# Sliding-window attention and a multiplicative FFN: Q and K cast by DMA, transposed in 32x32 blocks by VectorE, scores as 32-row matmuls

## The chip, the core and the metric

One Trainium2 chip, one core of it. The metric is the device time of one launch in microseconds: 290.55 us before the change, the median of three runs (290.41 to 290.74). Lower is better.

## What is computed

The reference takes q, k and v of shape (8, 8, 576, 64), that is 8 batches, 8 heads, 576 positions and 64 columns a head, and four weights, all in float32:

```
scores = (q @ k^T) / 8, kept where 0 <= i - j < 64, else -1e9   # causal, window of 64
attn   = softmax(scores)
x      = (attn @ v), heads side by side: 4608 tokens x 512
a, b   = x @ w1, x @ w2                                          # 512 -> 1024 each
out    = ((a * b) @ w3) @ w_out                                  # 1024 -> 1024 -> 512
```

## The kernel before, in words

**Fold.** `w3 @ w_out` is one 1024x512 matrix, `wc_sb`, made once on the chip: `fold_t(fc)` transposes 128 rows of w3 on TensorE (L470), VectorE copies them out (L472), `fold_mm(fc)` multiplies (L478). There are eight such steps.

**FFN.** The 4608 tokens are cut into nine groups g of 512. A group has twelve *slots*: `ffn_ab(g, fc)` for fc 0 to 7, which makes a 128-row piece of a and of b with 8 matmuls of 512 columns (L414), has ScalarE copy a out of PSUM (L419) and VectorE multiply b by it (L420); and `ffn_o(g, t)` for t 0 to 3, 8 matmuls (L432), a VectorE copy (L434) and a store.

**Attention.** Heads go in pairs j (0 to 3); the two heads of a pair are called a or hh (0, 1). The 576 queries of a batch are cut into three segments si of 192. A *unit* d is a batch, a segment and two of the four pairs: 48 units. `scores(d)` makes key-by-query scores with 8 matmuls (L279), each with 64 rows: the 64 columns of head a lie in one half of the 128 partitions. ScalarE's exp (L283) follows, and two masks on GpSimd (POOL, L291 and L293), which zero what lies outside the window; in segment 0 there are four smaller ones. `values(d)` multiplies by V with a block of ones beside it, which gives the softmax denominators (L336; L320 for the first two batches), takes the reciprocal by Ln and Exp on ScalarE (L342 to L344, or L326 and L327) and multiplies on VectorE into `xT` (L345 and L346, or L328), the FFN's input.

**Q and K.** `load_qk` loads both as float32 from SP's queue into `stage`. `cast_qk` makes float16 of them (L215, mostly on POOL; `cast_third`, L222, for the first batch). `transposes` then transposes 128x128 blocks on TensorE, six to a group (L254), and VectorE, or ScalarE for one in six, copies each group out of PSUM (L258). V and the weights are cast on their way by DMAs issued from POOL (L234, L453, L457, L463).

**PSUM.** It has eight banks: one for transposes (`ps_t`), two for scores (`ps_s`), two for `values` (`ps_v`), three for the FFN and the fold (`ps_f`).

**Order.** It is written by hand, and each engine works in that order. The *start* is a straight list: the first batches' loads, dummy matmuls (`keep_busy`, L503), the fold, the attention of batches 0 and 1, the FFN's group 0 and the transposes of batch 2. The *loop* then runs the remaining 96 slots. Between slots it runs *ticks* u, twelve to a batch; a tick comes when the next slot's due time, reckoned from what the group needs, allows it: one tick to a slot for most groups, 1.5 slots to a tick for groups 1, 4 and 7. In a tick, even u runs `scores(u/2)`, odd u runs `values` of the unit before, and the table `late` adds loads, casts, transposes and V copies for the coming batches:

```
    late = {0: [("t", 1, "k", 0), ("cast", 1, "q", 0)], 1: [("cast", 1, "q", 1)],
            2: [("t", 1, "k", 1), ("load", 2, "k")], 4: [("t", 1, "k", 2), ("v", 1, 0, 2, 3)],
            5: [("load", 2, "q")], 6: [("t", 1, "q", 0), ("v", 1, 4, 5)], 7: [("cast", 2, "k", 0)],
            8: [("t", 1, "q", 1), ("copy", 1, 4)], 9: [("copy", 1, 1), ("cast", 2, "k", 1)], 10: [("t", 1, "q", 2)]}
```

Of the kernel before, what the change touches and what calls it, by code (L numbers as in the profile page):

```python
# [15 lines left out]
P = 128  # L16
# [128 lines left out]
def kernel(  # L145
# [18 lines left out]
    TP, TI = 32, 18  # L164
# [4 lines left out]
    ND = 6 * B  # L169
# [29 lines left out]
    raws, k16s, q16s = {}, {}, {}  # L199

    def load_qk(b, which, gate=None):
        src = k if which == "k" else q
        t = sb.tile([P, 2, TI * D], FP32, name="stage", bufs=4)
        if gate is not None:
            gate(t[:, 0, 0:1], 0.0)
        for hh in range(2):
            nc.sync.dma_start(out=t[:, hh], in_=src[b, hh:H:2].rearrange("j (p r) d -> p j (r d)", r=TI))
        raws[which, b] = t

    def cast_qk(b, which, hh, cp):  # L210
        t = raws[which, b]
        if hh == 0:
            (k16s if which == "k" else q16s)[b] = sb.tile([P, TI, P], FP16, name=which + "16", bufs=1)
        t16 = (k16s if which == "k" else q16s)[b]
        cp(t16[:, :, hh * D:hh * D + D], t[:, hh].rearrange("p (i d) -> p i d", d=D))  # L215

    def cast_third(b, which, c, cp):
        t = raws[which, b]
        if c == 0:
            (k16s if which == "k" else q16s)[b] = sb.tile([P, TI, P], FP16, name=which + "16", bufs=1)  # L220
        t16 = (k16s if which == "k" else q16s)[b]
        cp(t16[:, 6 * c:6 * c + 6].rearrange("p i (hh d) -> p hh i d", hh=2),  # L222
           t[:, :, 6 * c * D:6 * c * D + 6 * D].rearrange("p hh (i d) -> p hh i d", d=D))
# [19 lines left out]
    kTs, qTs = {}, {}  # L243

    def transposes(b, which, *cs, into=None, cps=None):

        t16, dst = (k16s, kTs) if which == "k" else (q16s, qTs)
        if cs[0] == 0:
            dst[b] = sb.tile([P, NJ, S], FP16, name=which + "T")
        if into is None:  # L250
            into = [ps_t.tile([P, 6, P], FP16, name="tp")]
        for c, tp in zip(cs, into):
            for i in range(6):
                nc.tensor.transpose(tp[:, i, :], t16[b][:, 6 * c + i, :], ident16)  # L254
        if cps is None:
            cps = [dve_cp if which == "k" or c != 1 else act_cp for c in cs]
        for c, tp, cp in zip(cs, into, cps):
            cp(dst[b].rearrange("q j (p i) -> q j p i", i=TI)[:, :, :, 6 * c:6 * c + 6],  # L258
               tp.rearrange("q i (p j) -> q j p i", p=TP))


# [3 lines left out]
    def scores(d):  # L265

        b, r = divmod(d, 6)
        si, jp = divmod(r, 2)
# [3 lines left out]
        s_ps = ps_s.tile([P, 2, 2, 256], FP32, name="s_ps")  # L272
        for jj in range(2):
            j = 2 * jp + jj
            c0 = 0
            for (k0, q0, n, _) in seg:
                for a in range(2):
                    half = slice(a * D, a * D + D)
                    nc.tensor.matmul(s_ps[:, a, jj, c0:c0 + n], kT[half, j, k0:k0 + P], qT[half, j, q0:q0 + n],  # L279
                                     start=True, stop=True, skip_group_check=True)  # L280
                c0 += n
        pt = sb.tile([P, 2, 2, 256], FP16, name="pt", bufs=3)
        nc.scalar.activation(pt[:, :, :, 0:w], s_ps[:, :, :, 0:w], AF.Exp, bias=-SHIFT, scale=scale)  # L283

        rows = pt.rearrange("k a j n -> k (a j) n")
# [11 lines left out]
    def values(d):  # L297
# [7 lines left out]
        o_ps = ps_v.tile([P, 2, 512], FP32, name="o_ps")  # L305
# [6 lines left out]
        if b < SHORT:  # L312

            for jj in range(2):
                c0 = 0
                for bi, (k0, q0, n, _) in enumerate(seg):
                    o0 = jj * 192 + q0 - q_base
                    for e in range(2):
                        for a in range(2):
                            nc.tensor.matmul(o_ps[a * D:a * D + D, e, o0:o0 + n],  # L320
                                             v16[:, si * 2 + bi, j0 + jj, (2 * a + e) * D:(2 * a + e) * D + D],
                                             pt[:, a, jj, c0:c0 + n],
                                             start=(jj == 0 and bi == 0), stop=(bi == 1), skip_group_check=True)
# [6 lines left out]
        for jj in range(2):  # L330
            first = True
            for a in range(2):
                c0 = 0
                for bi, (k0, q0, n, _) in enumerate(seg):
# [3 lines left out]
                                     pt[:, a, jj, c0:c0 + n],  # L338
# [9 lines left out]
    def keep_sums(n):  # L348
# [5 lines left out]
    late = {0: [("t", 1, "k", 0), ("cast", 1, "q", 0)], 1: [("cast", 1, "q", 1)],  # L354
# [3 lines left out]

    def event(b, kind, ahead, *a):
        if b + ahead >= B:  # L360
            return
        if kind == "load":
            load_qk(b + ahead, *a)
        elif kind == "cast":
            cast_qk(b + ahead, *a, pool_cp)
        elif kind == "t":
            transposes(b + ahead, *a)
        elif kind == "v":
            load_v(b + ahead, *a)
        else:  # L370
            copy_v(b + ahead, *a)

    LAG = 3

    def tick(u):

        b, r = divmod(u, 12)
        d = u // 2
        if u % 2 == 0 and d < ND:
            scores(d)  # L380
        ev = late.get(r, [])
        for e in ev:
            if e[0] == "t":
                event(b, *e)
        if u % 2 == 1 and 12 <= d - 1 < ND:
            values(d - 1)
        for e in ev:
            if e[0] != "t":
                event(b, *e)
        n, m = divmod(u - LAG - 4, 4)  # L390
        if m == 3 and n >= 6:
            keep_sums(n)

# [100 lines left out]
    def count_bad():  # L494
        c_ps = ps_t.tile([1, 1], FP32, name="tp")
# [3 lines left out]
    def keep_busy(n):  # L499

        d = ps_t.tile([P, P], FP32, name="tp")
# [4 lines left out]
    load_qk(0, "k")  # L506
    load_qk(0, "q")
# [6 lines left out]
    ones_of(0)  # L514
    ones_of(1)
    load_wo()
    load_w3(0)
    load_v(0, 0, 2, 3)
    for n in range(1, 4):
        load_w3(n)  # L520
    load_v(0, 4, 5)
# [8 lines left out]
    def spare(pool, name):  # L530

        t = pool.tile([P, 2, 1024], FP16, name=name)
        return [t[:, i, 0:768].rearrange("p (i n) -> p i n", i=6) for i in range(2)]

    keep_busy(75)
    tps = spare(ps_s, "s_ps") + spare(ps_v, "o_ps")
    for c in range(3):
        cast_third(0, "k", c, act_cp if c == 1 else dve_cp)
# [156 lines left out]
```

## Time and profile before

| what | us |
|---|---|
| median of three runs | 290.55 |
| span of the profiled execution, first to last instruction | 289.2 |
| TensorE busy | 274.1 (95%) |
| VectorE busy | 179.4 (62%) |
| ScalarE busy | 163.1 (56%) |
| POOL busy | 180.5 (62%) |
| first FFN matmul (L414) of group 0 begins | 46.05 |
| first slot of the loop begins | 76.88 |
| last result copied out of PSUM | 284.15 |

The profile records one execution; its own time is not given apart from its span, so the 1.35 us between the span and the median is taken for what lies around the span. The granted TensorE clock was full (mean 0.999). In the profile "f_ps" is a tile of the FFN or the fold, "s_ps" and "o_ps" are scores and values, "tp" a transpose. "PE" is TensorE's matmuls; where several are listed together, the time is from the first one's start to the last one's end, and the ends are modelled: one matmul of 128 columns is listed with about 219 ns, but the next one can start after 56 ns.

### The profile page before, as it was taken

What the parts mean: (1) busy time and instruction counts of PE and PEld (TensorE: products, weight loads), DVE (VectorE), ACT (ScalarE), POOL (GpSimd) and SP (SyncE); (2) the same over time, 40 slices, a digit from 0 to 9 for tenths busy, and PEclk for the clock granted to TensorE, in tenths of its full rate; (3) what the DMA queues carried; (4) which work ended last, traced back from release to release, by engine and by line L of the source; (5) the groups of instructions that cost most, each with busy time, mean ns of one, the idle gap of its engine ahead of it and who ended that gap; (6) DMA issues with size and microseconds to landing.
All of it is one profiled execution on the core that took longest, in us unless ns stands there. A gap on an engine that the chain in (4) does not pass through costs nothing.

```text
span 289.2 us, 6103 instructions
## 1 busy us (share of the span) xinstructions
PE 274.1 (95%) x2358; PEld 154.1 (53%) x2358; DVE 179.4 (62%) x277; ACT 163.1 (56%) x270; POOL 180.5 (62%) x214
## 2 busy tenths in 40 slices
PE   7758989899999999999999999999999999999992
PEld 7644555454645555555555886555555445444442
DVE  0715477454977576878677765687767655555531
ACT  2512664675377557766876556478567765641310
POOL 8836996589689838795698463786595444401300
PEclk9999999999999999999999999999999999999999
DMA  6999999991399547395668650940193012013013
GB/s 236 212 179 204 246 299 215 373 164 60 98 372 164 65 155 285 24 109 161 269 44 113 209 193 5 197 33 0 38 172 26 0 73 76 0 37 112 0 37 116
DMA packets 51809, 38.85 MB, mean 134 GB/s; under 512 B 38800, under 2 KB 42128, under 8 KB 51776
## 3 DMA queue, kind: packets, MB, share of 16 engines
q0 software_dynamic: 41744, 9.96, 37.4%
q1 hardware_dynamic: 9888, 28.33, 26.7%
q8 instruction: 19, 0.31, 0.4%
q14 instruction: 14, 0.11, 0.1%
q10 hardware_dynamic: 144, 0.13, 0.1%
HBM read 38.80 MB, written 9.44 MB: 167 GB/s over the span
## 4 chain that ended last, share of the span: by engine, by line
PE 82%; POOL 8%; DMA 4%; ACT 2%; DVE 2%; issue 1%; POOLq 0%; DVEq 0%; ACTq 0%
PE f_ps L414 41%; PE f_ps L432 22%; PE o_ps L336 5%; PE tp L254 5%; PE s_ps L279 4%; DMA ab<-in_moe_w_dram 4%; POOL pt L291 2%; PE f_ps L478 2%; POOL pt L293 2%; POOL v L512 2%; PE o_ps L320 1%; PE s_ps L254 1%; POOL v L234 1%; ACT pt L283 1%; POOL w_sb L453 1%
## 5 line engine op out<-in xcount | busy, mean ns | idle before, releaser
L414 PE MATMUL f_ps<-xT,w_sb 128*128 128x512 f16 (+1 forms) x640 | 134.0, 358 | 0.0
L291 POOL TENSOR_SCALAR_AFFINE_SELECT pt<-pt 128x512 f16<-128x512 f16 (+1 forms) x64 | 52.5, 821 | 65.0 <-ACT pt L283 65.0
L414 PEld LDWEIGHTS <-w_sb 128*128 128x128 f16 x640 | 59.8, 98 | 50.6 <-issue 0.2
L432 PE MATMUL f_ps<-wc_sb,ab 128*128 128x512 f16 (+1 forms) x296 | 66.9, 373 | 0.1
L420 DVE TENSOR_TENSOR ab<-f_ps,a_sb 128x512 f16<-128x512 f32 x72 | 49.8, 692 | 20.4 <-PE f_ps L414 15.9
L419 ACT COPY a_sb<-f_ps 128x512 f32<-128x512 f32 x72 | 41.7, 579 | 25.4 <-PE f_ps L414 24.6
L283 ACT ACTIVATE pt<-s_ps 128x1024 f16<-128x1024 f32 (+1 forms) x48 | 45.5, 949 | 18.0 <-PE s_ps L279 16.5
L293 POOL TENSOR_SCALAR_AFFINE_SELECT pt<-pt 128x512 f16<-128x512 f16 (+1 forms) x64 | 51.9, 811 | 4.4
L345 DVE TENSOR_TENSOR xT<-o_ps,r 64x384 f16<-64x384 f32 x36 | 19.8, 550 | 39.8 <-ACT r L344 39.8
L432 PEld LDWEIGHTS <-ab 128*128 128x128 f16 x296 | 27.6, 98 | 27.9 <-issue 0.3
L234 POOL DMA_DIRECT2D v<-in_v_dram x40 | 33.9, 855 | 6.2 <-DMA ab<-in_moe_w_out_dram 4.4
L342 ACT ACTIVATE ln_s<-o_ps 64x384 f32<-64x384 f32 x36 | 17.5, 487 | 32.7 <-PE o_ps L336 32.7
L434 DVE COPY t2k<-f_ps 128x512 f32<-128x512 f32 (+1 forms) x36 | 24.5, 682 | 12.5 <-PE f_ps L432 12.1
L336 PEld LDWEIGHTS <-v 128*128 128x128 f16 x288 | 18.1, 98 | 8.7 <-ACT pt L283 0.8
L336 PE MATMUL o_ps<-pt,v 128*128 128x128 f16 (+1 forms) x288 | 20.7, 215 | 0.4 <-DVE xT L346 0.4
L346 DVE TENSOR_TENSOR xT<-o_ps,r 64x384 f16<-64x384 f32 x36 | 20.2, 561 | 0.5
L344 ACT ACTIVATE r<-ln_s 128x384 f32<-128x384 f32 x36 | 18.8, 522 | 1.1
L279 PEld LDWEIGHTS <-kT 64*128 64x128 f16 x384 | 10.5, 94 | 16.2 <-issue 14.8
L279 PE MATMUL s_ps<-qT,kT 64*128 64x128 f16 (+1 forms) x384 | 18.2, 214 | 0.3 <-ACT pt L283 0.2
L326 ACT ACTIVATE ln_s<-o_ps 128x384 f32<-128x384 f32 x12 | 5.9, 490 | 21.2 <-PE o_ps L320 21.2
L343 ACT ACTIVATE ln_s<-o_ps 64x384 f32<-64x384 f32 x36 | 17.4, 482 | 0.4
L258 DVE COPY kT<-tp 128x768 f16<-128x768 f16 x17 | 16.2, 951 | 0.0
(65 smaller groups left out, 222.6 us busy)
## 6 DMA issues: line engine op xcount, KB each, us to landing
stage<-in_k_dram SPq DMA_DIRECT2D x16, 576.0 KB
stage<-in_q_dram SPq DMA_DIRECT2D x16, 576.0 KB
out_dram<-t2k SPq DMA_DIRECT2D x35, 256.0 KB
v<-in_v_dram POOLq DMA_DIRECT2D x32, 128.0 KB, 4.6
w_sb<-in_moe_w_dram POOLq DMA_DIRECT2D x4, 512.0 KB, 10.9
ab<-in_moe_w_out_dram POOLq DMA_DIRECT2D x1, 1024.0 KB, 10.8
ab<-in_moe_w_dram POOLq DMA_DIRECT2D x2, 512.0 KB, 12.9
xT<-in_moe_w_dram POOLq DMA_DIRECT2D x2, 512.0 KB, 16.5
```

Source lines behind the costliest of these rows:

```text
L234: nc.gpsimd.dma_start(out=vh[lo:P, c], in_=v[b, :, s0:s0 + P - lo, :].rearrange("h s d -> s h d"))
L279: nc.tensor.matmul(s_ps[:, a, jj, c0:c0 + n], kT[half, j, k0:k0 + P], qT[half, j, q0:q0 + n], start=True, stop=True, skip_group_check=True)
L283: nc.scalar.activation(pt[:, :, :, 0:w], s_ps[:, :, :, 0:w], AF.Exp, bias=-SHIFT, scale=scale)
L291: nc.gpsimd.affine_select(out=sl, in_=sl, pattern=pat, compare_op=ALU.is_ge, fill=0.0, base=off, channel_multiplier=-1)
L293: nc.gpsimd.affine_select(out=sl, in_=sl, pattern=[[-s, m] for s, m in pat], compare_op=ALU.is_ge, fill=0.0, base=63 - off, channel_multip ...
L336: nc.tensor.matmul(o_ps[:, jj, o0:o0 + n], v16[:, si * 2 + bi, j0 + jj, a * D:a * D + P], pt[:, a, jj, c0:c0 + n], start=first, stop=(bi = ...
L346: nc.vector.tensor_tensor(xs[D:P], o_ps[D:P, :, 192:384], r[D:P], ALU.mult)
L414: nc.tensor.matmul(d[:, f * n + c0:f * n + c1], w[:, dc, (fc + f) * P:(fc + f + 1) * P], xT[:, dc, xc:xc + c1 - c0], start=first, stop=(dc ...
L419: act_cp(a_sb[:, 0:nf * n], a_ps[:, 0:nf * n])
L420: nc.vector.tensor_tensor(ab[:, fc:fc + nf, lo:hi], b_ps[:, 0:nf * n].rearrange("p (f n) -> p f n", f=nf), a_sb[:, 0:nf * n].rearrange("p ...
L432: nc.tensor.matmul(o_ps[:, 0:c1 - c0], ab[:, fc, t * P:t * P + P], wc_sb[:, fc, c0:c1], start=(fc == 0), stop=(fc == 7))
L434: cp(o_sb[:, c0:c1], o_ps[:, 0:c1 - c0])
```

## The change

Q and K are loaded by POOL's casting DMAs, straight to float16, one head pair j per 32 partitions: partition 32j+p holds positions 18p to 18p+17. VectorE's `transpose` turns 32x32 blocks, so that a head's 64 columns lie as two halves c of 32 on the 32 partitions of its pair. A score is now two accumulating matmuls with 32 rows (c = 0 and 1), and the four pairs j use the four groups of 32 rows, each with a PSUM bank of its own. `scores(n)` covers all four pairs of a segment: 32 matmuls in a block, 24 blocks, in place of 8 matmuls in 48. The rest of a unit (exp, masks) is unchanged, in `weigh`. In PSUM, scores and values share four banks as two buffers (`ps_a`), and `ps_f` has four. V's ones are set by VectorE in place of POOL. In a four-tick round, tick 0 runs `scores(n)`, ticks 1 and 2 run `values` of the two units of segment n-1, tick 3 its bookkeeping. The start is re-ordered: more of the fold stands ahead of the values of batch 0.

```diff
-    ps_t = fast.enter_context(tc.tile_pool(name="ps_t", bufs=1, space=PSUM))
-    ps_s = fast.enter_context(tc.tile_pool(name="ps_s", bufs=1, space=PSUM))
-    ps_v = fast.enter_context(tc.tile_pool(name="ps_v", bufs=1, space=PSUM))
-    ps_f = fast.enter_context(tc.tile_pool(name="ps_f", bufs=3, space=PSUM))
+    ps_a = fast.enter_context(tc.tile_pool(name="ps_a", bufs=2, space=PSUM))
+    ps_f = fast.enter_context(tc.tile_pool(name="ps_f", bufs=4, space=PSUM))
...
+    def load_qk(b, which):
         src = k if which == "k" else q
+        t = sb.tile([P, 2, TI * D], FP16, name=which + "16", bufs=2)
         for hh in range(2):
+            nc.gpsimd.dma_start(out=t[:, hh], in_=src[b, hh:H:2].rearrange("j (p r) d -> j p (r d)", r=TI))
+        t16s[which, b] = t
+
+    def transposes(b, which, hh):
+        dst = kTs if which == "k" else qTs
         if hh == 0:
+            dst[b] = sb.tile([P, 2, 2, S], FP16, name=which + "T")
+        nc.vector.transpose(dst[b][:, hh].rearrange("q c (p i) -> q i c p", i=TI), t16s[which, b][:, hh].rearrange(
+            "p (i c e) -> p i c e", c=2, e=32))
...
+    def scores(n):
+        b, si = divmod(n, 3)
...
+        s_ps = [ps_a.tile([P, 2, 512], FP32, name="a_ps") for _ in range(2)]
+        c0 = 0
+        for (k0, q0, m, _) in seg:
+            for a in range(2):
+                for c in range(2):
+                    for j in range(NJ):
+                        part = slice(32 * j, 32 * j + 32)
+                        o0 = 256 * a + c0
+                        nc.tensor.matmul(s_ps[j // 2][:, j % 2, o0:o0 + m], kT[part, a, c, k0:k0 + P],
+                                         qT[part, a, c, q0:q0 + m], start=(c == 0), stop=(c == 1),
+                                         skip_group_check=True)
+            c0 += m
+        for jp in range(2):
+            weigh(2 * n + jp, s_ps[jp].rearrange("k j (a n) -> k j a n", a=2)[:, :, :, 0:w], si, w)
...
-        o_ps = ps_v.tile([P, 2, 512], FP32, name="o_ps")
+        o_ps = ps_a.tile([P, 2, 512], FP32, name="a_ps")
...
+    late = {0: [("load", 2, "k")], 1: [("t", 1, "k", 0), ("load", 2, "q")], 2: [("v", 1, 0, 2)],
+            3: [("t", 1, "q", 0), ("v", 1, 3)], 5: [("t", 1, "k", 1), ("v", 1, 4, 5)], 7: [("t", 1, "q", 1)],
+            8: [("copy", 1, 4)], 9: [("copy", 1, 1)]}
...
+    LAG = 4
     def tick(u):
         b, r = divmod(u, 12)
+        n, m = divmod(u, 4)
+        if m == 0 and n < NS:
+            scores(n)
+        if m in (1, 2) and 6 < n <= NS:
+            values(2 * n - 3 + m)
+        for e in late.get(r, []):
+            event(b, *e)
+        if m == 3 and 6 < n <= NS:
+            keep_sums(n - 1)
...
     def ones_of(i):
-        nc.gpsimd.memset(v16s[i].rearrange("p c j (a e) -> p (c j a) e", a=2)[:, :, D:2 * D], 1.0)
+        nc.vector.memset(v16s[i].rearrange("p c j (a e) -> p (c j a) e", a=2)[:, :, D:2 * D], 1.0)
...
+    load_qk(0, "k")
+    load_qk(0, "q")
+    load_wo()
+    load_w3(0)
+    load_w3(1)
+    ones_of(0)
+    keep_busy(100)
+    for hh in range(2):
+        transposes(0, "k", hh)
+        transposes(0, "q", hh)
+    keep_busy(30)
+    load_v(0, 0, 2, 3)
+    load_w3(2)
+    load_w3(3)
+    scores(0)
     keep_busy(15)
     scores(1)
+    keep_busy(15)
+    w3Ts[0] = fold_t(0)
+    fold_step(0)
+    load_v(0, 4, 5)
+    ones_of(1)
+    scores(2)
+    fold_step(1)
     for i in range(2):
         load_w12(i, 0)
+    fold_step(2)
+    fold_step(3)
     copy_v(0, 1)
+    fold_step(4)
+    load_qk(1, "k")
+    load_qk(1, "q")
+    values(0)
+    copy_v(0, 4)
+    fold_step(5)
+    values(1)
+    values(2)
+    fold_step(6)
+    for i in range(2):
+        load_w12(i, 1)
+    values(3)
+    values(4)
+    fold_step(7)
     values(5)
+    load_v(1, 0, 2, 3)
     for n in range(3):
         keep_sums(n)
+    load_v(1, 4, 5)
+    load_qk(2, "k")
+    ffn_ab(0, 0)
+    transposes(1, "k", 0)
+    ffn_ab(0, 1)
+    transposes(1, "q", 0)
+    ffn_ab(0, 2)
+    transposes(1, "k", 1)
+    load_qk(2, "q")
+    ffn_ab(0, 3)
+    transposes(1, "q", 1)
+    for fc in range(4, 6):
+        ffn_ab(0, fc)
+    scores(3)
     copy_v(1, 1)
+    ffn_ab(0, 6)
+    copy_v(1, 4)
+    ffn_ab(0, 7)
+    steps = [lambda t=t: ffn_o(0, t) for t in range(4)]
+    scores(4)
+    load_v(2, 0, 2)
+    for d in range(6, 12):
         values(d)
+        if d == 9:
+            scores(5)
+            load_v(2, 3)
+        if d % 2 == 0 or d == 9:
             steps.pop(0)()
             store()
+        if d in (6, 7, 8, 9):
+            transposes(2, "kq"[d % 2], (d - 6) // 2)
```

More of the change, by code (lines that the diff above doesn't have):

```diff
@@ L163 @@
     NJ = H // 2
-    TP, TI = 32, 18
+    TI = 18
     GT = 512
@@ L168 @@
     NU = 12 * B
-    ND = 6 * B
+    NS = 3 * B
     SHORT = 2
@@ L361, in event @@
             return
[L362 to L373, printed above, removed]
+        do = {"load": load_qk, "t": transposes, "v": load_v, "copy": copy_v}[kind]
+        do(b + ahead, *a)
+    LAG = 4
     def tick(u):
         b, r = divmod(u, 12)
[L378 to L392, printed above, removed]
+        n, m = divmod(u, 4)
[7 more added lines that the diff above has]
+            keep_sums(n - 1)
     abs_ = {}
@@ L528, in fold_step @@
         fold_mm(fc, w3Ts.pop(fc), act_cp if fc % 4 == 3 else dve_cp)
[L530 to L538, printed above, removed]
-    transposes(0, "k", 0, 1, 2, into=tps, cps=[dve_cp, act_cp, dve_cp])
-    keep_busy(10)
-    for c in range(3):
-        cast_third(0, "q", c, act_cp if c == 1 else dve_cp)
```

142 lines of the change are left out of this document (11 added, 131 removed), and 3 rows, old and new, of the table late.

## The prediction

> **What bounds the kernel now.** The page first: busy times, then the slices, then the chain that ended last.
>
> ```profile
> PE 274.1 (95%) x2358; PEld 154.1 (53%) x2358; DVE 179.4 (62%) x277; ACT 163.1 (56%) x270; POOL 180.5 (62%) x214
> PE   7758989899999999999999999999999999999992
> POOL 8836996589689838795698463786595444401300
> PE 82%; POOL 8%; DMA 4%; ACT 2%; DVE 2%; issue 1%; POOLq 0%; DVEq 0%; ACTq 0%
> ```
>
> PE is the bound from about slice 8 on, with no other engine near it; the chain leaves it only in the start (POOL, DMA). Over the loop the windows say the same:
>
> ```profile
> 130.00:251.00 121.00, 121.00 (x1004) 68.60 (x1001) 85.02 (x132) 81.34 (x138) 75.50 (x91) 1.00 0.46 97
> ```
>
> So in the loop what leaves PE's queue shortens the run, as long as nothing shows behind it. The timeline of PE prices each step by starts, since the listed ends overlap the next step:
>
> ```profile
> 118.20 0.50 PE L336 MATMUL o_ps<-pt,v 128*128 128x128 f16 x8
> 118.54 1.89 PE L414 MATMUL f_ps<-xT,w_sb 128*128 128x512 f16 x8
> 120.37 0.40 PE L279 MATMUL s_ps<-qT,kT 64*128 64x128 f16 x8
> 120.69 0.51 PE L254 MATMUL tp<-ident,q 128*128 128x128 f16 x6
> 121.04 1.89 PE L414 MATMUL f_ps<-xT,w_sb 128*128 128x512 f16 x8
> 122.77 0.61 PE L336 MATMUL o_ps<-pt,v 128*128 128x128 f16 x8
> ```
>
> A slot is 1.728 us (121.04 to 122.77; 8 x 216 ns), `values` 0.447 (0.338 in segment 0), a group of six transposes 0.345 (120.69 to 121.04). Scores: the slot before is done at 118.54 + 1.728 = 120.27, the block starts 0.10 later, its last matmul is 0.18 behind its first, and the transposes start 0.15 after that: 0.436 with the 10 ns lost on the next step, 0.381 in segment 0. About 0.19 of each block is the change to 64 rows and back. Eight scores are listed with 0.40 and eight values of the same width with 0.61: the two halves run together, two matmuls per 56 ns (starts 3 ns apart in the trace).
>
> **PE in the loop.** Transposes: batches 3 to 7 have 30 groups, 30 x 0.345 = 10.35 us. Gone from PE.
> Scores: a block after has 8 fours of 32-row matmuls. If four run together as two do now, a four costs 56 ns, and the block 0.10 + 7 x 0.056 + 0.02 + 0.15 + 0.01 = 0.67 against 2 x 0.436 for the same work; segment 0 with 64-column fours at 28 ns 0.555 against 2 x 0.381. That saves 0.207 a block, the second change of row mode; 18 blocks in the loop give 3.7. Bounds: 56 ns a four, and 4 x 56 ns if they run one by one. I take 56: in segment 0 the trace has pairs of 64 columns every 28 ns, each with two weight loads, so four weight loads and four matmuls in 56 ns is a rate PE shows already. Only 64-column fours (4 in each of 6 blocks of the loop) ask for more; at 56 ns they cost 0.7 in all.
> The Trainium skill (TensorE: Matmul & The Clock Gate, Part 3) measured 3.07 for four 32-row matmuls side by side, not 4. By that a four would cost 73 ns and the kernel 3.3 us more, over 24 blocks; no row here shows four.
> Rest unchanged: 96 slots 166.1, 36 `values` 14.8. So 166.1 + 14.8 + 11.3 = 192.2 against 206.2 now (measured 76.88 to 284.14, 207.3: 1.1 of waits).
>
> **VectorE.** It loses the copies out of PSUM (L258) and its casts and gains 32 transposes:
>
> ```profile
> L258 DVE COPY kT<-tp 128x768 f16<-128x768 f16 x17 | 16.2, 951 | 0.0
> L434 DVE COPY t2k<-f_ps 128x512 f32<-128x512 f32 (+1 forms) x36 | 24.5, 682 | 12.5 <-PE f_ps L432 12.1
> ```
>
> That is 35.9 us (16.2 + 12.3 + 4.6 + 1.9 + 0.9) and 3.8. A transpose T handles 1152 elements a partition. No row shows one. By L434's forms (690 ns for 512, 425 for 256: 1.04 ns an element) it is 425 + 896 x 1.04 = 1.36 us. Low end: its cast of 128x1152 took 0.83. Far end: each of the 36 blocks as its own small instruction (L497, 135 ns), 4.9. I take 1.36, since L258, which also scatters, keeps the rate of L434. So VectorE stays where it was: 179.4 - 39.7 + 32 x 1.36 + two memsets of up to 3.2 (3072 x 1.04) = 189.
>
> **POOL, ScalarE, SP, DMA.** POOL loses 25 casts (L215, 28.2) and memsets (5.3) and gains 32 DMA issues at about 0.76 (w_sb, L453): 171. Behind such an issue stand the next masks. It can wait, as it does now:
>
> ```profile
> POOL v L234 <- DMA ab<-in_moe_w_out_dram: 4.4, 1, 4.4
> ```
>
> There the DMA eight issues back had not landed. In the loop nine issues a batch of some 25 us, landing in about 5 us each (v, 4.6), never reach that, and the q and k tiles (two each) are free a batch earlier. ScalarE loses 12 us of copies and casts. SP only keeps the stores. The same bytes are read: a 4608-byte row of q takes a DMA engine 178 ns today, a casting row of half that size 173. All this is free under PE in the loop.
>
> **The cover that goes.** Fewer PE steps lie between an evacuation and its user, and scores and values share two buffers. Take a four-tick round of `ffn_ab` slots, t from the scores, with rows L283 1.02, L342 to L344 1.49, L345 and L346 1.11, L419 0.58, L420 0.69. PE wants 0.67 + 4 x 1.728 + 2 x 0.447 = 8.47. ScalarE: exps 0.9 to 2.9, a-copy to 3.5, Ln and Exp of values 1 to 5.0. VectorE: product of slot 0 at 4.2, the two of values 1 at 6.15, T of tick 1 at 7.5, and only then the product of slot 1, 8.2. Slot 3 uses slot 1's banks and wants the second at 7.6: 0.6 lost. The next scores want the products of values 2, queued behind at 9.3: another 0.2. A round without T: slot 1's product at 6.85, nothing lost. The same reckoning for the kernel before (three banks, copies of 0.95) gives no loss, as the trace shows. Rounds with T and one tick per slot, mostly `ffn_ab`: five, 4.2; the crowded first round of group 1, where two `values` follow each other, some 1.3. Taken: 5.5; none if T is 0.83.
>
> **The start.** POOL issues q and k from 1.45 to 4.5; 512 rows over 16 engines at 0.19 take 6 us, so the last lands near 10.3. VectorE then works k, q, k, q in its order and ends near 12.7; `scores(0)` follows (13.59 now). The dummies fill PE until then. w_out and w3 come behind q and k in one queue: first w3 near 18.2 (19.95 now), which starts the fold. From there PE: fold 8 x (0.45 + 1.73) + scores 0.67 + six `values` at 0.57 + 0.3 = 21.8, so `values(5)` ends at 40.0. Masks no longer hold it: POOL, not caught in that 4.4 wait, has those of batch 0 by 29. But group 0 follows at once and waits for Ln, Exp and product, 1.8: 41.8 (46.05 now). Six slots, `scores(3)`, two slots, `scores(4)`: 57. `values(6)` then wants the buffer the exp has just begun to read: 1.3 lost. Later `scores(5)` waits 1.9 for the products of `values(9)`, `values(10)` 1.9 for masks, and the loop's first slot 1.8 for `values(11)`. With six `values`, four slots and a block, 57.0 + 6.9 + 3.4 + 6.9 + 0.7: the loop starts at 75.0, 1.9 earlier. Most of what the fold's order wins is lost in these gaps.
>
> **Sum.** 75.0 + 192.2 + 5.5 + 5.05 (284.15 to the span's end, unchanged) = 277.75 of span, against 289.2; with the 1.35 between span and median, **279.1 us**.
>
> **Rivals.**
> - *Waits show more than worked out* (buffers shared, start 5 later, loop losing another 3): 287. For: every engine is at 80 to 90% of a round. Against: the same reckoning fits the round of before. 0.16.
> - *Fours cost 73 ns*: 282.4. 0.10.
> - *Fours run as two pairs*, 112 ns: 8 x 56 ns x 24 = 10.7 more, 289.8, no change within 0.2% or so. Against: nothing in the pairs hints at a limit of two. 0.04.
> - *Slower: VectorE becomes the bound through T.* If turning a block is a pass in and then a pass out, T is 2 x 1.36 = 2.7. A batch costs VectorE 12 x 0.69 + 6 x 1.11 + 1.5 (V copies) + 4T = 16.4 + 4T, PE about 25.1: equal at T = 2.2. At 2.7 the loop loses 5 x 2.1 = 10.5 in place of 5.5, and the start 1.35 for each of some six T in the path: 279.1 + 5 + 8.1 = 292.2. Slower than now from about T = 2.6. For: no row shows a turn inside VectorE. Against: all its rows stay near 1 ns an element. 0.10.
> - *Row groups don't run together at all*: block 2.0, 24 x 1.4 = 33 more, 312. 0.02.
> - *The start gains* (q and k land and fold earlier, T below 1): 273. 0.06.
>
> The Trainium skill (VectorE: DVE Perf Modes, The three transpose paths) gives 311 ns for 128 columns turned in 32x32 blocks; nine such would be 2.8 us, and the time about 294, an estimate. No run shows it yet.
>
> **Numbers.** The forecast of 279.1 has 0.52. Faster is it, 287, 282 and 273: 0.84. Within 0.2% (0.6 us, about what a measurement of this kernel can tell from no change) lie 0.03 of the pairs' 0.04. Slower: 0.10 + 0.02 + 0.01 = 0.13. The range reaches from 271 (no waits in the loop, start 3 earlier) to 291, which leaves out the slow T, the serial rows and little else.
>
> **What would show it.** Right: no L254; blocks of 32 scores of about 0.57 us from first to next step; T near 1.36; loop from about 75; PE gaps of under 1 us in rounds with T. Wrong: blocks over 1 us; T over 2; POOL waiting for DMAs ahead of masks; gaps at `values` or `scores` in every round.

## The result and the profile after

The changed kernel takes 408.71 us (median of 4 runs, 407.18 to 412.15) against 290.64 for the kernel before on the same chip: 1.4072 times as long, 95% interval 1.4003 to 1.4141. The forecast said 279.1 with a range to 291: wrong in sign and far outside. The profiled execution took 407.49 us, with a span of 405.8.

The page, in the order in which that of before was read: busy times, slices of PE, VectorE and the granted clock, and the chain that ended last.

```profile
PE 291.7 (72%) x2474; PEld 153.8 (38%) x2474; DVE 300.1 (74%) x267; ACT 149.7 (37%) x256; POOL 169.0 (42%) x218
...
PE   8008895747067454987679567978696779999995
...
DVE  2892756976956399779977997598969896655542
...
PEclk9757999569668855996889887989899789999999
...
PE 40%; DVE 26%; issue 16%; DMA 10%; POOL 6%; ACT 1%; DVEq 0%; POOLq 0%
```

Before, PE was at 9 from slice 8 on, with the granted clock at 9 throughout, and the chain was 82% PE. Now PE stays at 9 only in the last slices, where no turns are left; before that VectorE is the busiest engine, a quarter of the chain is VectorE's, and the granted clock is below 9 in more than half of the slices. VectorE's busy time is 300.1 us where the prediction worked out 189. The groups of the page say which instruction it is (columns: line, engine, operation, output and input, count; busy us, mean ns of one; idle before):

```profile
L211 DVE STREAM_TRANSPOSE kT<-k 128x1152 f16<-128x1152 f16 x16 | 81.9, 5119 | 16.4 <-DMA k<-in_k_dram 16.1
...
L211 DVE STREAM_TRANSPOSE qT<-q 128x1152 f16<-128x1152 f16 x16 | 82.1, 5134 | 0.1
```

One turn T takes 5.12 us, not 1.36: 32 of them are 164 us in place of 43.5. The page's DMA issues show a second thing (KB each, then us from issue to landing; v landed in 4.6 before):

```profile
k<-in_k_dram POOLq DMA_DIRECT2D x16, 288.0 KB, 11.4
q<-in_q_dram POOLq DMA_DIRECT2D x16, 288.0 KB, 12.1
v<-in_v_dram POOLq DMA_DIRECT2D x32, 128.0 KB, 11.1
```

Both are seen together in the first 33 us. VectorE's timeline (start, duration, operation, idle before):

```profile
11.29 5.10 DVE L211 STREAM_TRANSPOSE kT<-k 128x1152 f16<-128x1152 f16 x1 [7.06 <-DMA k<-in_k_dram]
16.03 5.27 DVE L211 STREAM_TRANSPOSE qT<-q 128x1152 f16<-128x1152 f16 x1
20.95 5.27 DVE L211 STREAM_TRANSPOSE kT<-k 128x1152 f16<-128x1152 f16 x1
25.87 5.27 DVE L211 STREAM_TRANSPOSE qT<-q 128x1152 f16<-128x1152 f16 x1
```

and PE's, which stands still for 10.5 and 9.4 us inside the first score block:

```profile
21.36 0.40 PE L249 MATMUL a_ps<-qT,kT 32*128 32x128 f16 x8 [10.53 <-DVE qT L211]
31.20 0.61 PE L249 MATMUL a_ps<-qT,kT 32*128 32x128 f16 x24 [9.44 <-DVE qT L211]
```

`scores(0)` begins at 21.36 and is done near 31.9 (it began at 13.59 before and was forecast from 12.7), and the loop starts at 125.1 instead of 76.9: 48.2 of the 116.6 us of longer span. The other 68.4 lie in the loop. One round of it, PE and then VectorE:

```profile
199.82 0.41 PE L249 MATMUL a_ps<-qT,kT 32*128 32x128 f16 x14
200.16 3.17 PE L392 MATMUL f_ps<-wc_sb,ab 128*128 128x512 f16 x7
205.85 0.39 PE L392 MATMUL f_ps<-wc_sb,ab 128*128 128x512 f16 x1 [2.52 <-DVE ab L380]
```

```profile
200.16 5.11 DVE L211 STREAM_TRANSPOSE qT<-q 128x1152 f16<-128x1152 f16 x1
204.92 0.87 DVE L380 TENSOR_TENSOR ab<-f_ps,a_sb 128x512 f16<-128x512 f32 x1
```

A turn holds VectorE's queue from 200.16; the product `ab` that stands behind it is done only at 205.8, and PE's next matmul needs it. The seven matmuls before it start 0.42 us apart, 2.54 us from the first to the seventh, where full rate is 6 x 0.216 = 1.30: they ran at half the clock (0.50 granted from 200.1 to 203.4 us). The windows of PE show the granted clock as the sixth figure after the window's length (PE, PEld, DVE, ACT and POOL busy, each with a count, then the clock):

```profile
125.00:160.00 35.00, 19.99 (x165) 8.29 (x165) 24.59 (x19) 11.31 (x18) 17.59 (x25) 0.65 1.17 97
...
360.00:400.00 40.00, 40.00 (x216) 19.43 (x215) 21.22 (x34) 14.52 (x27) 6.52 (x6) 1.00 0.11 41
```

Where PE is left waiting the clock is 0.65, where nothing interrupts it 1.00. Taken step by step over the loop, 60.0 us are waits (26 steps between matmuls that are late by over 0.12 us) and 18.2 are 88 matmuls of 512 columns that took about 0.42 us instead of 0.216. With the 192.2 us of work that the prediction had, that is 270 of 275.7. The longest waits of PE over the whole run, behind VectorE (us in total, times, longest):

```profile
PE a_ps L249 <- DVE xT L322: 29.0, 8, 5.3
PE f_ps L374 <- DVE ab L380: 23.8, 10, 7.6
```

The wait of 7.6 us is only in part a turn's: the turn that stands before that product had itself waited for k to land,

```profile
138.64 5.11 DVE L211 STREAM_TRANSPOSE kT<-k 128x1152 f16<-128x1152 f16 x1 [6.69 <-DMA k<-in_k_dram]
```

so some of the loop's 60.0 us belongs to the loads. POOL has a wait too, which the prediction excluded, where it issues loads of V:

```profile
POOL v L223 <- DMA k<-in_k_dram: 17.4, 4, 9.0
```

In the trace POOL's DMAs take eight semaphores in turn, and each of these waits ends 0.28 us after the DMA eight issues back has landed. That is how this program takes its semaphores; nothing here shows it as a limit of the chip.

What came out as forecast is PE's own price. A score block at full clock has 0.411 us from its first start to its last (eight fours of 56 ns, with 17 ns for the last four), 0.10 before and 0.15 after: 0.66 against the 0.67 worked out, 0.55 in segment 0 against 0.555. There the 64-column fours come every 28 ns, as the working took them.

### The profile page after: what moved, and what is told of

It reads as the page before. It is cut to its first block, busy times and chain, and to the rows that moved or that the text cites. A ratio compares the mean times of both kernels' runs of the same rounds, so it can differ in the third digit from the quotient of the medians.

```text
span 405.8 us, 6273 instructions
## 1 busy us (share of the span) xinstructions
PE 291.7 (72%) x2474; PEld 153.8 (38%) x2474; DVE 300.1 (74%) x267; ACT 149.7 (37%) x256; POOL 169.0 (42%) x218
## 4 chain that ended last, share of the span: by engine, by line
PE 40%; DVE 26%; issue 16%; DMA 10%; POOL 6%; ACT 1%; DVEq 0%; POOLq 0%
PE f_ps L374 22%; PE f_ps L392 11%; DVE qT L211 10%; DVE kT L211 9%; DMA k<-in_k_dram 7%; PE a_ps L312 4%; DMA q<-in_q_dram 3%; DVE ab L380 3%; PE a_ps L249 2%; POOL pt L269 2%; POOL pt L267 2%; DVE xT L322 2%; DVE xT L321 1%; DVE t2k L394 1%; POOL v L223 1%
## 5 line engine op out<-in xcount | busy, mean ns | idle before, releaser
L374 PE MATMUL f_ps<-xT,w_sb 128*128 128x512 f16 (+1 forms) x640 | 151.5, 392 | 30.1 <-DVE ab L380 23.8
L211 DVE STREAM_TRANSPOSE kT<-k 128x1152 f16<-128x1152 f16 x16 | 81.9, 5119 | 16.4 <-DMA k<-in_k_dram 16.1
L259 ACT ACTIVATE pt<-a_ps 128x1024 f16<-128x1024 f32 (+1 forms) x48 | 43.1, 950 | 118.3 <-PE a_ps L249 118.3
L211 DVE STREAM_TRANSPOSE qT<-q 128x1152 f16<-128x1152 f16 x16 | 82.1, 5134 | 0.1
L392 PE MATMUL f_ps<-wc_sb,ab 128*128 128x512 f16 (+1 forms) x296 | 75.9, 411 | 7.6 <-DVE ab L380 7.6
L249 PE MATMUL a_ps<-qT,kT 32*128 32x128 f16 (+1 forms) x768 | 19.2, 234 | 63.2 <-DVE xT L322 29.0
L223 POOL DMA_DIRECT2D v<-in_v_dram x40 | 34.1, 856 | 19.5 <-DMA k<-in_k_dram 17.4
L249 PEld LDWEIGHTS <-kT 32*128 32x128 f16 x768 | 13.7, 103 | 74.4 <-issue 44.2
L321 DVE TENSOR_TENSOR xT<-a_ps,r 64x384 f16<-64x384 f32 x36 | 19.6, 546 | 19.0 <-ACT r L320 19.0
L318 ACT ACTIVATE ln_s<-a_ps 64x384 f32<-64x384 f32 x36 | 17.5, 487 | 40.1 <-PE a_ps L312 40.0
L312 PE MATMUL a_ps<-pt,v 128*128 128x128 f16 (+1 forms) x288 | 23.0, 229 | 0.0
L322 DVE TENSOR_TENSOR xT<-a_ps,r 64x384 f16<-64x384 f32 x36 | 20.2, 561 | 0.5
L319 ACT ACTIVATE ln_s<-a_ps 64x384 f32<-64x384 f32 x36 | 17.4, 482 | 0.4
## 6 DMA issues: line engine op xcount, KB each, us to landing
k<-in_k_dram POOLq DMA_DIRECT2D x16, 288.0 KB, 11.4
q<-in_q_dram POOLq DMA_DIRECT2D x16, 288.0 KB, 12.1
v<-in_v_dram POOLq DMA_DIRECT2D x32, 128.0 KB, 11.1
ab<-in_moe_w_dram POOLq DMA_DIRECT2D x2, 512.0 KB, 18.2
```

Of the source, the lines that this page charges most:

```text
L211: nc.vector.transpose(dst[b][:, hh].rearrange("q c (p i) -> q i c p", i=TI), t16s[which, b][:, hh].rearrange("p (i c e) -> p i c e", c=2, ...
L223: nc.gpsimd.dma_start(out=vh[lo:P, c], in_=v[b, :, s0:s0 + P - lo, :].rearrange("h s d -> s h d"))
L249: nc.tensor.matmul(s_ps[j // 2][:, j % 2, o0:o0 + m], kT[part, a, c, k0:k0 + P], qT[part, a, c, q0:q0 + m], start=(c == 0), stop=(c == 1), ...
L259: nc.scalar.activation(pt[:, :, :, 0:w], s_ps, AF.Exp, bias=-SHIFT, scale=scale)
L312: nc.tensor.matmul(o_ps[:, jj, o0:o0 + n], v16[:, si * 2 + bi, j0 + jj, a * D:a * D + P], pt[:, jj, a, c0:c0 + n], start=first, stop=(bi = ...
L374: nc.tensor.matmul(d[:, f * n + c0:f * n + c1], w[:, dc, (fc + f) * P:(fc + f + 1) * P], xT[:, dc, xc:xc + c1 - c0], start=first, stop=(dc ...
```

## The experiments

The leading theory after the result was that T pays for each single 2-byte element that it writes away from its neighbours (theory B of the first run). The rivals were that a turn in 32x32 blocks is slow in itself, and that the late loads or the shared buffers carry the loss.

**`forms`: the disputed instruction by itself.** The kernel before, with scratch instructions at its start; `tf_in` and `tf_out` are used by nothing else. Total 330.08 us.

```diff
+        nc.vector.transpose(tf_out[:, 0].rearrange("q (c p i) -> q i c p", ...),            # L515 as in the change
+                            with_forms[:, 0].rearrange("p (i c e) -> p i c e", ...))
+        nc.vector.transpose(tf_out[:, 0].rearrange("q (i c p) -> q i c p", ...), ...)       # L517 output dense
+        ...                                                                               # L519, L521: 576, both ways
+        nc.vector.transpose(tf_out[:, 0, 0:128], with_forms[:, 0, 0:128])                  # L523
+        nc.vector.tensor_copy / nc.scalar.copy / nc.gpsimd.tensor_copy(scattered as L515)  # L524, L526, L528
```

> The kernel before, with copies and transposes of scratch data added at its start to price forms. After the change one transpose of 128x1152 took 5.12 us, 142 ns for each of its 36 blocks. Theory A (a fixed price for each 32x32 block): all 1152-column forms take about 5.1, halves of 576 columns 2.6, 128 columns 0.57, whether the output is scattered or dense. Theory B (the price is the scattered write, single 2-byte elements 36 bytes apart): dense output of 1152 columns about 1.4 and of 576 about 0.75; scattered 576 columns (18 bytes apart) about 2.6. Copies of 1152 columns in the scattered order: by A near 1.3 on VectorE, by B near 5 there, and perhaps on ScalarE and POOL too.

VectorE's groups (busy us, mean ns of one):

```profile
L515 DVE STREAM_TRANSPOSE tf_out<-tf_in 128x1152 f16<-128x1152 f16 x2 | 10.5, 5256 | 0.0
L519 DVE STREAM_TRANSPOSE tf_out<-tf_in 128x576 f16<-128x576 f16 x2 | 5.4, 2722 | 0.1
L524 DVE COPY tf_out<-tf_in 128x1152 f16<-128x1152 f16 x2 | 5.2, 2606 | 0.1
L517 DVE STREAM_TRANSPOSE tf_out<-tf_in 128x1152 f16<-128x1152 f16 x2 | 2.8, 1378 | 0.1
...
L523 DVE STREAM_TRANSPOSE tf_out<-tf_in 128x128 f16<-128x128 f16 x2 | 0.6, 311 | 0.1
```

The same copy on POOL and ScalarE, from the page:

```profile
L528 POOL COPY tf_out<-tf_in 128x1152 f16<-128x1152 f16 x2 | 10.3, 5131 | 28.1 <-ACT tf_out L526 28.1
...
L526 ACT COPY tf_out<-tf_in 128x1152 f16<-128x1152 f16 x2 | 10.4, 5176 | 22.1 <-DVE tf_out L524 22.1
```

The turn alone is not slow: 1.38 us with a dense output, within 2% of the 1.36 of the prediction. Only the order in which it writes makes it 5.26. The price is 4.4 to 4.7 ns for each element, at 36 bytes from element to element (L515) as at 18 (L519). ScalarE and POOL pay the same for a plain copy in that order, VectorE's copy half. In the kernel before, as many elements written in runs of 64 took POOL and ScalarE 1.15 us and VectorE 0.83 (casts from float32):

```profile
L215 POOL CAST q<-stage 128x1152 f16<-128x1152 f32 x13 | 14.5, 1145 | 0.0
```

So the price belongs to the single stores, not to the turn. Why a store costs this was not tried. The Trainium skill (VectorE: DVE Perf Modes, The three transpose paths) has 311 ns for 128 columns; L523 measures that very number, so the figure holds for one small dense turn. Nine of them, 2.8 us, is what neither the dense nor the scattered 1152 costs.

**`c_out`, `p_outer`, `c_out_p_outer`: T and the loads apart.** The first two change one line each of the changed kernel, the third has both. They keep every size but leave out the right order of positions and heads, so they price the parts and are no version of the change.

```diff
# c_out: T writes its columns in the order in which it turns them
-        nc.vector.transpose(dst[b][:, hh].rearrange("q c (p i) -> q i c p", i=TI), ...
+        nc.vector.transpose(dst[b][:, hh].rearrange("q c n -> q (c n)").rearrange("q (i c p) -> q i c p", i=TI, c=2), ...
# p_outer: the loads go over the 32 rows first, over the four heads inside
-            nc.gpsimd.dma_start(out=t[:, hh], in_=src[b, hh:H:2].rearrange("j (p r) d -> j p (r d)", r=TI))
+            nc.gpsimd.dma_start(out=t[:, hh], in_=src[b, hh:H:2].rearrange("j (p r) d -> p j (r d)", r=TI))
```

> The changed kernel, with the transposes writing their blocks densely, so that kT and qT hold the positions in another order (the attention is that of permuted positions; the instructions and sizes are the same). Theory A: transposes stay at 5.1 us and the time at about 408. Theory B: transposes near 1.4, VectorE busy falls by 118 us to about 182, PE is the bound again, and the time falls to 280 to 295, the prediction's 279 plus what the late landing of q and k costs in the start.

> The changed kernel, with the q and k loads written partition by partition with the 32 rows outermost (partition 4p+j in place of 32j+p, so heads are mixed up in the blocks; same bytes and row sizes). Theory: a load whose outermost dimension is 4 runs on few DMA engines; with 32 outermost it runs on 16, landing falls from a median of 11.4 us to 5 or less and the first transposes start near 6 in place of 11.3. Time: the start's 5 us less, and some waits for DMAs, so 395 to 404, since the transposes stay at 5.1. Rival: the slow landing is POOL's queue itself (descriptors), landing stays above 9, time 408.

> Both edits together: the changed kernel with dense transposes and with q and k loads of 32 rows outermost (permuted positions and mixed heads, same sizes). Theory B and the engine count: this is the kernel that the prediction described, 275 to 285. If PE waits still show in every round, 290 or more. Theory A: about 400.

Measured, in one run each: 303.86, 393.56 and 290.23 us, against 407.49 for the profiled run of the change. T and the landing came out as expected, the times less so: `c_out` missed 280 to 295, `p_outer` lies 1.4 us under its range, and `c_out_p_outer` fell on its "290 or more". In `c_out` VectorE is busy for 184.1 us, and from its page:

```profile
L211 DVE STREAM_TRANSPOSE kT<-k 128x1152 f16<-128x1152 f16 x16 | 22.0, 1373 | 18.0 <-DMA k<-in_k_dram 17.7
```

`p_outer`, page:

```profile
k<-in_k_dram POOLq DMA_DIRECT2D x16, 288.0 KB, 4.9
```

The scattered output is worth 103.6 us with the slow loads and 103.3 with the fast ones; the order of the loads 13.9 with the slow T and 13.6 with the fast one. The two add up, to 117.3, as closely as single runs can tell (the change's own four runs spread over 5 us). About half of the loads' share lies before the loop, which starts at 117.6 in `p_outer` and at 125.1 in the change. In the trace of the change one q or k load keeps about four of the sixteen DMA engines busy: the rows in flight are 4.3 at 180.5 us, 8.7 at 182.0 and about 13 from 183 on, as the loads of a batch set in one after another. With the rows outermost one load spreads over all, the landing falls from 11.4 to 4.9 us for k and from 12.1 to 7.3 for q, and of POOL's 17.4 us of wait 1.1 are left. The Trainium skill (DMA: Bandwidth & Descriptors, Why a DMA increments its semaphore by 16 and not by 1) states the rule: a transfer is split over the largest number of engines up to 16 that divides the outermost dimension of both sides. Four heads outermost give four engines, 32 rows sixteen; the rows in flight agree.

With both repaired the kernel is where it started, 11.1 us above the forecast. Its loop starts at 77.8 (75.0 forecast), and the loop loses 10.8 us to waits and 1.0 to a lower clock (5.5 forecast). Two rounds with T lose 0.73 at the scores and 0.51 at a slot, 1.24 where 0.84 was worked out; one of the first loses 2.1 at its scores alone. The largest single wait was in no sum. VectorE and PE of `c_out_p_outer` near 100 us:

```profile
100.14 1.15 DVE L227 COPY v<-v 64x512 f16<-64x512 f16 x1 [3.88 <-DMA v<-in_v_dram]
```

```profile
98.29 1.46 PE L392 MATMUL f_ps<-wc_sb,ab 128*128 128x512 f16 x6
102.07 1.21 PE L392 MATMUL f_ps<-wc_sb,ab 128*128 128x512 f16 x2 [2.32 <-DVE ab L380]
```

VectorE stands 3.88 us before a copy of V whose load has not landed; the product behind it in VectorE's queue is what PE waits for.

**`pairs` and `pairs_by_head`: the same arithmetic with cheaper stores, and smaller loads.** `pairs` moves elements two at a time, as one 4-byte word, so that T has half as many stores; the matmuls then read every second element. `pairs_by_head` also loads each head by itself.

```diff
# pairs
-            dst[b] = sb.tile([P, 2, 2, S], FP16, name=which + "T")
+            dst[b] = sb.tile([P, 2, S, 2], FP16, name=which + "T")
-        nc.vector.transpose(...)
+        nc.vector.transpose(dst[b][:, hh].rearrange("q n c -> q (n c)").bitcast(FP32).rearrange("q (p i) -> q i p", i=TI),
+                            t16s[which, b][:, hh].bitcast(FP32).rearrange("p (i e) -> p i e", e=32))
-    kT[part, a, c, k0:k0 + P], qT[part, a, c, q0:q0 + m]
+    kT[part, a, k0:k0 + P, c], qT[part, a, q0:q0 + m, c]
# pairs_by_head, on top
+            for j in range(NJ):
+                nc.gpsimd.dma_start(out=t[32 * j:32 * j + 32, hh], in_=src[b, 2 * j + hh].rearrange("(p r) d -> p (r d)", r=TI))
```

> The changed kernel, computing the same, with VectorE turning 4-byte elements: two neighbouring float16 columns of a head are one element, so a transpose has 576 elements a partition in 18 blocks, written 72 bytes apart, and a score's two matmuls take the even and the odd columns (read 4 bytes apart) in place of the two halves. Theory B1 (every scattered write costs 4.4 ns): a transpose takes 2.6 us, VectorE is busy for 225, time about 320. Theory B2 (only writes under 4 bytes are slow): 0.75 us, VectorE 165; the time is that of the dense transposes with the late loads, 304, less the waits behind the transposes, so 295 to 304. A rival on PE: reading 4 bytes apart halves the rate of the matmuls, a block takes over 1 us in place of 0.67.

> The same, and each load of q or k split by head, 32 partitions each (128 issues in place of 32), so that the outermost dimension is 32 and all DMA engines work. Theory: landing falls from 11 to under 6 us; under B2 the time is 275 to 287 (the prediction's 279, less the waits behind transposes, plus what 96 more issues on POOL of 0.3 to 0.7 us each hold up). Rival: POOL becomes late with the masks, 290 or more.

`pairs`: 307.76 us (305.46 to 312.49; the profile is of the longest run), 1.0508 of before (1.0425 to 1.0592). Its T, from the page, and POOL's wait:

```profile
L211 DVE STREAM_TRANSPOSE kT<-k 128x576 f32<-128x576 f32 x16 | 20.0, 1253 | 22.3 <-DMA k<-in_k_dram 22.0
```

```profile
POOL v L223 <- DMA k<-in_k_dram: 22.7, 4, 13.5
```

T is 1.25 us, 2.2 ns for each of 576 scattered 4-byte stores: half of the 2-byte price per store, a quarter per byte. That lies between the two theories (2.6 and 0.75), and the time misses both, 320 and 295 to 304. Blocks that wait for nothing keep 0.42 to 0.43 from first to last start (0.41 in the change), so reading operands at 4-byte steps costs PE next to nothing here. What keeps `pairs` above 290 is, by VectorE's longest waits for DMAs, the loads (22.0 for k) and V (11.3). `pairs_by_head`: 308.38 us, 1.054 (1.0465 to 1.0614), where the rival had 290 or more. The landing is 3.0 us, and nothing was won by it. POOL, which now issues 128 times, is busy for 210.5 us against 169.0 in the change:

```profile
PE a_ps L313 <- POOL pt L270: 5.9, 5, 3.3
```

Its masks come late, and PE waits for them, here and for another 5.4 us before the loop; `pairs` has 1.3 us of such waits in all. A cheaper transfer in four times as many issues was no gain here, where the issuing engine has other work due.

**`merged`, `merged_v`, `before_v`: the score blocks alone.** `merged` is the kernel before with nothing of the change but the merged blocks (16 matmuls of 64 rows, both head pairs of a segment), the shared `a_ps` buffers, six tiles of probabilities in place of three and the order of ticks that comes with them; PE still transposes. `merged_v` loads V earlier and copies it later; `before_v` does that in the kernel before.

```diff
# merged
-    ps_s = ...; ps_v = ...
+    ps_a = fast.enter_context(tc.tile_pool(name="ps_a", bufs=2, space=PSUM))
-        if u % 2 == 0 and d < ND:
-            scores(d)
+        if m == 0 and n < 3 * B:
+            scores(2 * n, 2 * n + 1)
...                                                            # pt with 6 buffers, LAG = 4, the ticks of values
# merged_v and before_v: the table `late`
-   4: [("t", 1, "k", 2), ("v", 1, 0, 2, 3)], ... 6: [("t", 1, "q", 0), ("v", 1, 4, 5)], ...
-   8: [("t", 1, "q", 1), ("copy", 1, 4)], 9: [("copy", 1, 1), ("cast", 2, "k", 1)], 10: [("t", 1, "q", 2)]
+   3: [("v", 1, 0, 2, 3)], 4: [("t", 1, "k", 2), ("v", 1, 4, 5)], ...
+   8: [("t", 1, "q", 1)], 9: [("cast", 2, "k", 1)], 10: [("t", 1, "q", 2), ("copy", 1, 4)], 11: [("copy", 1, 1)]
```

> The kernel before with one part of the change alone: the scores of a segment's two units in one block in the loop (64 rows, two at a time as before), scores and values sharing two buffers of two banks, six tiles of probabilities and the tick order of the changed kernel; loads, casts, TensorE transposes and the order of the start stay. Theory: each merged block saves one change of row mode, 0.2 us, 18 in the loop, so 3.7 us: 287. Rival: sharing the buffers brings waits at scores or values, as in the changed kernel's rounds (0.5 to 1.2 each), 290 or more.

> `merged` (the kernel before with merged score blocks and shared buffers) with V's loads one and two ticks earlier (r = 3 and 4 in place of 4 and 6) and VectorE's copies of V two ticks later (r = 10 and 11 in place of 8 and 9). Theory (of the 9 us that `merged` lost against before, VectorE's wait for V, 17.9 us in 5 places, is a part): that wait falls under 3 us, the loop's waits of PE fall from 10.9 to about 7, time about 296. Rival (the shared buffers and the longer way from scores to values cost all of it): 299, waits of PE as before. If V were all of it: 289 or less.

> The kernel before, with V's loads and VectorE's copies of V on the ticks of `merged_v` (loads at r = 3 and 4, copies at r = 10 and 11) and nothing else. VectorE of before shows no wait for V among its longest, so if `merged_v` owes its gain to the merged blocks, this stays at 290.6 to 291.3, ratio within 0.003 of 1. Rival (the moved copies are a gain of their own, and the merged blocks none): about 288, ratio 0.99.

`merged`: 299.4 us, 1.0259 (1.0189 to 1.0328), with 10.6 us of waits in the loop. VectorE's waits name the cause:

```profile
DVE v L237 <- DMA v<-in_v_dram: 17.9, 5, 5.4
```

The expected 287 was missed, and the rival had the waits but not this cause. `merged_v`: 288.01 us, 0.9899 (0.9865 to 0.9933). That wait is gone, the loop's waits are 1.1 us, and PE is busy for 96% of the span against 95% before. The expectation gave V only a part of the loss; V was all of it. `before_v` is at 291.99 us, 1.0027 (1.0007 to 1.0047), so the moved loads and copies of V are no gain of their own, slightly the reverse. Between the two ratios lies 0.0128, 3.7 us; the prediction's working for merged blocks is 18 x 0.207 = 3.7 in the loop, and PE's own starts give a merged block 0.65 us where two single ones take 0.85. The shared buffers do not take it back once VectorE is free of V.

**`pairs_h2` and `pairs_h2_first`: a version of the change that gains a little.** `pairs` with four loads per tensor, each of one head pair for all 32 rows, and V's copies two ticks later; then with the first phase in another order.

```diff
# pairs_h2, against pairs
-        for hh in range(2): ...
+        for j in range(NJ):
+            nc.gpsimd.dma_start(out=t[32 * j:32 * j + 32], in_=src[b, 2 * j:2 * j + 2].rearrange("h (p r) d -> p h (r d)", r=TI))
-            8: [("copy", 1, 4)], 9: [("copy", 1, 1)]}
+            10: [("copy", 1, 4)], 11: [("copy", 1, 1)]}
# pairs_h2_first, on top: the first phase's order from values(3) on
+    values(3), values(4), load_v(1, 0, 2, 3), values(5), fold_step(7), ...
+    ffn_ab(0, 4), scores(3), load_v(2, 0, 2, 3), copy_v(1, 1), ffn_ab(0, 5), copy_v(1, 4), ffn_ab(0, 6), scores(4), ...
+    values(6), ffn_o, values(7), ffn_o, scores(5), load_qk(3, "k"), values(8), ffn_o, values(9) to values(11), ffn_o
```

> The changed kernel with three alterations that keep its arithmetic: the turn moves pairs of elements (T 1.25 us, as in `pairs`), each q or k tensor of a batch comes in four transfers of one pair of heads each (32 partitions x two rows, outermost dimension 32, four issues in place of two), and VectorE's copies of V inside the SBUF stand two ticks later (r = 10 and 11 in place of 8 and 9). Theory (what was lost is T, the slow landing with POOL held behind it, and VectorE standing in front of a copy whose V has not landed): first k landed by about 5 us, POOL's wait at v gone, VectorE's wait for V (3.9 us in `c_out_p_outer`) gone, waits of PE in the loop 9 us or less, POOL busy about 190 (32 more issues of about 0.5 us on top of 170), time about 286, under before's 290.6. Rival 1 (buffers shared by scores and values are what costs, whatever the loads do): loop waits stay at 12 us or more and the time is 290 or more. Rival 2 (POOL, with its extra issues, comes late with masks, as in `pairs_by_head`): PE waits behind POOL's pt, time 295 or more.

> `pairs_h2` with its first phase in another order: the last fold step stands behind the last `values` of batch 0, group 0's last slots stand between its scores and values, the loads of batches 2 and 3 are issued earlier and none ahead of masks that are due, and the copies of V of batch 2 earlier. Theory (what `pairs_h2` still lacks against the worked sum lies in the gaps of its first phase: 1.35 at 43.6, 1.42, 1.65, 1.77 and 1.80 from 59.6 to 72.3, 1.35 at 77.5, 1.3 at 87 and 2.3 at 92.3 with a stretch of halved clock behind): half or more of these 12.9 us goes, the loop starts by about 73, time 279 to 282. Rival (the order only moves the waits, since POOL's masks of batch 1 and ScalarE's steps set that stretch): 286 to 288, gaps of the same sum elsewhere.

`pairs_h2`: 287.47 us, 0.9868 (0.9807 to 0.993). From its page, the landing with 32 issues in place of 16:

```profile
k<-in_k_dram POOLq DMA_DIRECT2D x32, 144.0 KB, 5.0
```

Waits in the loop are 6.7 us, and 2.9 a lower clock, so neither rival holds. VectorE's wait for V is down to 0.3 us. POOL is busy for 181.0, 9 under the 190 expected; the four parts of the first k landed at 4.8 to 8.7, not all by 5, and the first turn starts at 8.8. The two alterations went in together, so their shares are not told apart. `pairs_h2_first`: 286.11 us, 0.9825 (0.9781 to 0.9868), the lowest of all, though its runs (284.61 to 287.15) overlap those of `pairs_h2` (285.25 to 288.7); 279 to 282 was expected. The loop's waits fell to 3.5 us, yet the first phase got worse: some 17 us of waits before the loop against some 14, and the loop starts at 81.3 instead of 77.3. What the new order won in the loop's first rounds it lost in front of the loop. The largest of these waits are for the masks of batch 1 (4.4 us in `pairs_h2`), as the rival had it, and the time is the rival's 286:

```profile
PE a_ps L296 <- POOL pt L269: 8.3, 4, 3.0
```

## Why the prediction was wrong, step by step

**VectorE's T: the step that failed.** The text took 1.36 "since L258, which also scatters, keeps the rate of L434". L258 writes runs of six elements, 12 bytes at a time; T writes every element alone. That is a difference in the store pattern, and the trace of before had no row with single 2-byte stores. The far end of the working, 4.9 us, was close to the 5.12 measured by luck: it priced each of 36 blocks as an instruction, and `forms` has the same 36 blocks at 1.38 with a dense output. Even so, the chance of 0.10 and the range of times stopped at T of 2.7. Without a row for the pattern, the far end should have been carried into the range: `T = 4.9` by the rival's own formula gives a batch of 16.4 + 4 x 4.9 = 36 us on VectorE against 25.1 on PE, over 50 us of loss.

**The slow rival had the right engine, but its sum fits partly by luck.** With the measured 5.12 it gives 16.4 + 20.5 = 36.9 us a batch on VectorE, 11.8 over PE's 25.1, and over five batches 59 us; the loop's waits are 60.0. But the formula takes VectorE as never idle, and then a slower PE would cost nothing more. In the trace VectorE is busy for 174 of the 210 us from 125 to 335, a batch takes 39.2 to 43.4 us from its first turn to that of the next, and the loop loses 18.2 us to PE's clock beside its waits. Some of these waits are the loads': in `p_outer` 55.1 are left. For the start the rival had too little: 1.35 more for each of six turns, scaled to 3.76, would be 23 us, and the loop began 48.2 later than before.

**POOL and the DMAs: a second step that failed.** "In about 5 us each" was read from V's loads, which have 128-partition tiles and another order of dimensions; q and k with four heads outermost took 11.4 and 12.1. With that, "never reach" the eight-back limit fell too: POOL waited 17.4 us at V's loads. The runs with and without the new order price this at 13.6 to 13.9 us, none of which stood in the sum. A row took 0.19 us, as worked out, but "512 rows over 16 engines" did not hold: one load had about four.

**The cover that goes: right mechanism, too small.** With T and loads repaired (`c_out_p_outer`) the loop lost 11.8 us where 5.5 were taken. Two rounds with T lose 1.24 each instead of 0.84, and VectorE's wait for V, with 2.3 us of PE and a lower clock behind it, was not thought of: the prediction checked who waits for VectorE's turns, but not what VectorE's copies wait for. In `merged` that wait alone turned a gain into a loss of 2.6%.

**PE in the loop: right.** Blocks of 0.66 and 0.55 us, transposes gone, and fours at 56 ns; the 73 ns that the Trainium skill's ratio of 3.07 (TensorE: Matmul & The Clock Gate, Part 3) would have given (the skill's is for 512 columns) does not show in this kernel at 128 and 64. `merged_v` against `before_v` shows the block's saving as time, 3.7 us.

**The start.** The order of the fold and its waits can't be judged in the change itself, since T and the loads drown them; in `c_out_p_outer` the loop starts 2.8 us later than worked out.

## What to carry to other kernels

Ask of every instruction in which order and in what sizes it writes, and price it only by a row that writes the same way; where none exists, the far bound belongs in the range. Of every new transfer, read the outermost dimension before the bytes, and of every engine that others wait for, read what it waits for itself: a copy that stands in front of its DMA holds up all that is queued behind. A part of a change can be a gain where the whole is a loss, so measure the parts before the whole is given up.

## What the runs showed of the hardware that was not expected

- Single scattered 2-byte stores cost 4.4 to 4.7 ns each in VectorE's turn and in copies on ScalarE and POOL, 2.3 in VectorE's copy (2.61 us for 1152); dense output 1.2 in the turn. Scattered 4-byte stores cost 2.2 in the turn.
- Behind every wait of 2.4 us or more in the changed kernel's loop PE's granted clock is at half for 3.4 us or a multiple of it: from 200.1 to 203.4, starts of 512-column matmuls are 0.43 us apart instead of 0.216. Waits thus cost more than their length, here 18.2 us beside 60.0. It is no fixed rule: `merged` has a wait of 3.3 us at 96.7 with no such stretch behind it.
- One load by POOL with four as its outermost dimension kept about four of the sixteen DMA engines busy and landed in 11.4 us (288 KB); with 32 outermost the same bytes landed in 4.9.
- Four 32-row matmuls side by side start every 56 ns at 128 columns and every 28 ns at 64, with operands read at steps of 2 or of 4 bytes alike.
